# Linear attention and a gated MLP in one kernel: two more blocks take g times w_out by seven quarter products, and the written order of the work is made anew

## The chip, the cores and the metric

The kernel runs on one core of one Trainium2 chip. The metric is device time in microseconds; shown are the median of three runs and one profiled execution. An engine is called by its name or by the profile's short one: TensorE (PE, its weight loads PEld), VectorE (DVE), ScalarE (ACT), GpSimd (POOL), SyncE (SP, which issues nearly all DMAs).

## The reference

q, k and v have 8 batches, 8 heads, 576 tokens and 64 columns. Attention is linear, with features of exponentials, and its output is the input of an MLP with 4608 tokens, 512 columns and 2048 hidden columns:

```
phi(x):  p = x @ w_phi;  p = p - max|p|;  [exp(p), exp(-p)]        # 64 -> 256
kv = phi(k)^T v;  z = sum phi(k);  x = (phi(q) kv) / (phi(q) z + 1e-6)
h = x @ w_in;  g = h * erf(softplus(h));  out = g @ w_out
```

All is float32 in and out. The kernel takes each large float32 product as three float16 ones (high by high, high by low, low by high).

## The kernel before, in words

**Blocks and units.** The 4608 tokens are nine blocks of 512 (`NS`): eight batches without their last 64 tokens, and a ninth of these tails. The 2048 hidden columns are four units (`NU`). A unit (s, u) of the MLP makes h for one block and one unit (`h_unit`, L1060) by a Strassen-like scheme: seven products of 256 by 256 quarters in place of eight (`product`, L1032), whose sums are formed while the banks of PSUM are drained (`snap`, `add`). The input forms of the seven products (`split`, L871) and the weight forms (`split_weights`, L593) are pairs of float16; the weight forms of units 1 to 3 are kept in DRAM (`wd`) and fetched for each block into four tiles `ws` (`fetch`, L555).

**The gate.** `erf_gate` (L1108) takes Softplus and Erf on ScalarE, multiplies h by the result on VectorE (L1130, L1125), and then makes the operand of the second product. For blocks below `OW` (0 to 5) that is a float16 cast on ScalarE (L1133) and a subtraction on VectorE (L1136), both of 1024 columns, twice for a unit. For blocks from `OW` on (6 to 8) `g_forms` (L1140) makes four sums of quarters (`mix_g`, L1159) and seven pairs of float16 (`split_g`: ScalarE's cast, VectorE's subtraction L1153), of 512 columns each, in tiles `gf`.

**The second product** of a block goes in two rounds r of two units each, a round in two half-rounds. Below `OW` a half-round is `o_piece` (L1264): two token tiles, for each two units of four weight rows of 512 columns by three terms, 48 calls of `mm` (L509), which issues two matmuls on the two halves of the array's columns. The sums of round 0 are drained, stored in DRAM (`part`) and fetched for round 1. From `OW` on it is `o_chunk` (L1203): seven quarter products in 14 chunks for a round, seven for a half-round, 84 calls of `mm` with 256 columns; seven drains for a round (L1241, L1244) go to four sums `oc` that stay in SBUF. Their weight forms are made once by `t_forms` (L1173) on GpSimd, kept in DRAM (`td`) and fetched for each round (L1213).

**Attention** of batch b goes in nine groups of four tiles of 128 tokens for each batch: projection (`project`, L726), the row maximum and subtraction (`front`, L674 and L685), exponentials, turning (`t_piece`, by TensorE up to pair 9, then by a DMA transpose), kv and the quotients (`kv_piece`, `n_piece`, L524), and the split of x for the MLP (`x_piece`). Attention of batch b+1 is laid between the units of block b, so from about 736 us on only the MLP is left.

**The order** is made by a planner (`Plan`) in the host program: each operation has a cost, a latency and a rank (the place in the stream, `plan.pos`, plus an offset), and a simulated run picks on each engine the ready operation of the lowest rank; the order that comes out is each engine's instruction order. The planner holds tiles in pools with quotas (`plan.kind`), models DMAs as one queue (`land`), keeps GpSimd operations apart from VectorE operations marked `port`, charges 92 ns for a change of TensorE's mode and lets operations of another mode wait (`stay`). Where TensorE would be idle over 600 ns it puts in filler matmuls (`warm`, L1406).

Of the kernel before, what the change touches and what calls it, by code (L numbers as in the profile page):

```python
# [38 lines left out]
EARLY = 2 * NPAIR  # L39
PE_TURNED = 10  # L40
SPEED = {}
STAY2 = 5000.0
N1 = 12
TWO = 36
# [3 lines left out]
GATE_AT = (2000.0, 2000.0, 2000.0)  # L48
X_POOL = (0, 9)
T_POOL = 4  # L50
# [4 lines left out]
HL_POOL = (12, 20)  # L55
LATE = 1000.0
LATE2 = 2500.0
N3 = 7
FIRST = 2
XS = 8  # L60
XT = 3
RES = 1
WS = 8
HB = 4
PO = 2
BIG = 20
HALF = 36
N0 = 6
N2 = 24
W_EARLY = 3  # L70
W_NS = 1600.0
# [5 lines left out]
XT_ACT = (0, 2)  # L77
WRS = 4
GATE_OFF = (3000.0, 3500.0, 4500.0)
W_FROM = 16  # L80
W_EACH = 7
W_MM = 14
W_OFF = 6000.0
W_AHEAD = 12000.0
X_AHEAD = 8000.0
SEVEN = 7
O_ODD = (0, 1, 1, 0, 1, 1, 0)
# [3 lines left out]
KPS = 5  # L91
# [4 lines left out]
AHEAD = 5000.0  # L96
# [3 lines left out]
LAND = 0.68  # L100
HOLE = 600.0
OW = 6
GF = 18
OC = 6
TW_FROM = 16
TW_STEP = 1
TW_POOL = 1
OW_ODD = (0, 0, 1, 1, 1, 2, 2)
OW_EVEN = (0, 0, 0, 0, 0, 0, 0)
GW_OFF = 500.0  # L110
# [7 lines left out]
TAIL = (6, 1)  # L118
OW_LAG = 0
M_POOL = ()  # L120
GL_POOL = 0, 0
SYNC = 1
URGENT = 5000.0
NEAR = 100.0
PORT_NS = 120.0
WINDOW = 0.7
PRINT = None
EXP_LN = "natural_log_exp_and_others"

# [17 lines left out]
class Op:  # L147
    __slots__ = ("eng", "cost", "done", "fn", "prio", "bufs", "succ", "unmet", "ready", "start", "mode", "seq", "land", "port", "slack", "need", "give", "stay", "after", "made", "late")


class Plan:


    def __init__(self):
        self.ops = []
        self.slots = {}
        self.free = {}
        self.group = {}
        self.quota = {}
        self.line = {}  # L160
        self.row = {}
        self.pos = 0.0
        self.slack = 0.0
        self.stay = STAY
        self.late = LATE

# [11 lines left out]
    def op(self, eng, cost, fn, r=(), w=(), done=None, off=0.0, mode=COLS, land=0.0, port=False, need=None, give=None):  # L178
# [6 lines left out]
        o.late = self.late  # L185
        o.done = cost + 120.0 if done is None else done
        o.prio = self.pos + off
        o.seq = len(self.ops)
        o.succ, o.unmet, o.ready, o.start = [], 0, 0.0, None
        o.bufs = []  # L190
        deps = {}
# [44 lines left out]
    def run(self, filler):  # L236
# [17 lines left out]
        def room(o):  # L254
            if o.seq not in rooms:
                rooms[o.seq] = find_room(o) if any(b.slot is None for b in o.bufs) else 0.0
            return rooms[o.seq]

        def find_room(o):
            at = 0.0  # L260
            ahead, taken = {}, {}
            for b in o.bufs:
                if b.slot is not None:
                    continue
# [32 lines left out]
        def window(o, s):  # L297

            if o.prio + URGENT < min((c.prio for c in cand["DVE"]), default=0.0):
                return True  # L300
            work, blocked = max(0.0, free["DVE"] - s), False
            for c in cand["DVE"]:
# [3 lines left out]
                if at is None or max(c.ready, at) > s + NEAR:  # L306
                    continue
# [4 lines left out]
            return not blocked or work >= WINDOW * o.cost  # L312

        while left:
            rooms.clear()
            starts = {}
            for e in engines:
                t = None
                for o in cand[e]:
# [8 lines left out]
                    if t is None or s < t:  # L328
                        t = s
                if t is not None:  # L330
                    starts[e] = t
            if not starts:
# [8 lines left out]
            if held and held is not o:  # L341
                held.ready = max(held.ready, t)
            if e == "PE" and free[e] and t - free[e] > HOLE:
# [9 lines left out]
            table = o.give or table  # L353
# [4 lines left out]
            if o.land:  # L358
                queue_free = max(queue_free, t + o.cost) + o.land
                done = max(done, queue_free - t + o.late, o.done + o.late - LATE)  # L360
            free[e] = t + cost
            if o.port:
                port[e] = t + cost
                if e == "DVE":
# [3 lines left out]
            for b in o.bufs:  # L368
                if b.slot is None:
                    k = b.kind  # L370
# [7 lines left out]
                if b.left == 0:  # L378
                    used[b.kind] -= 1
                    self.free[self.group[b.kind]].append((b.end, b.slot))  # L380
            for n in o.succ:
# [5 lines left out]
                if n.unmet == 0:  # L387
                    cand[n.eng].append(n)
            order.append((t, o.seq, lambda o=o: self.emit(o)))
# [7 lines left out]
def favor_attention_moe(ctx: ExitStack, tc: tile.TileContext, qk, vp, wphi, w_in, w_out, out):  # L397
# [51 lines left out]
    for i in range(4 * NU):  # L449
        plan.slot("wd", f"wd{i}", pd.tile([P, HW], F32, tag=f"wd{i}", name=f"wd{i}"))  # L450
# [7 lines left out]
    plan.kind("wt", "big", (("wt",), WT))  # L458
# [3 lines left out]
    plan.kind("ws", "big", (("ws",), WS))  # L462
# [24 lines left out]
    whole("mb", 4, [P, GT], F32)  # L487
# [17 lines left out]
    op(SP, 450, lambda: nc.sync.dma_start(wst.t, wphi), w=[wst], done=2500)  # L505
# [42 lines left out]
    def wform(u, f):  # L548
# [3 lines left out]
        b = wforms[u][f // 2]  # L552
        return b, f, lambda hl, j: b.t.bitcast(F16).rearrange("p (f h j n) -> p f h j n", f=2, h=2, j=2)[:, f % 2, hl, j, :]

    def fetch(u):  # L555
        wforms[u] = []
        for i in range(4):
            b, d = buf("ws"), wstored[u][i]
            keys = range(2 * i, min(2 * i + 2, FORMS))
            n = 512 * len(keys)  # L560
            op(SP, 430, lambda b=b, d=d, n=n: nc.sync.dma_start(b.t[:, :n], d.t[:, :n]), r=[d], w=[(b, (f, j)) for f in keys for j in range(2)], done=2500, land=1300 * len(keys) * LAND, off=-W_AHEAD)
            wforms[u].append(b)

    def single(src, eng, st, f, port=True):
        word = lambda k: st.t.bitcast(I32).rearrange("p (e w) -> p e w", w=2)[:, :, k]
        for c, (d, s) in enumerate(src):
            op(SP, 430, lambda d=d, s=s: nc.sync.dma_start(d(st), s), w=[(st, c)], done=2500, land=2600 * LAND / len(src))
# [7 lines left out]
    def load_weight():  # L575
# [3 lines left out]
        plan.pos += W_OFF  # L579
# [13 lines left out]
    def split_weights(u, j):  # L593
        if u >= RES and j == 0:
            wforms[u] = [buf("ws") for _ in range(4)]
# [26 lines left out]
        if u >= RES and j == 1:  # L622
            wstored[u] = []
            for i in range(4):
                d = buf("wd")
                d.left += 1
                w = wforms[u][i]
                n = 512 * min(2, FORMS - 2 * i)
# [834 lines left out]
```

## Time and profile before

| | |
|---|---|
| median of three runs | 947.59 us (947.37 to 947.97) |
| the profiled execution | 945.1 us, span 943.3 us |
| TensorE matmul busy | 931.6 us, 99% of the span |
| TensorE weight load | 792.1 us, 84% |
| VectorE | 756.8 us, 80% |
| ScalarE | 716.9 us, 76% |
| GpSimd | 225.9 us, 24% |
| HBM | 119.50 MB read, 30.15 MB written |

The span is from the first instruction to the last; 1.8 us of the profiled execution lie around it. Matmuls are pipelined and their ends are modelled, so what one costs is read from the distance of starts and not from its own length. Busy time of the other engines is the union of their instructions.

### The profile page before, as it was taken

Reading aid. Unit: us, or ns where it says so; the run is one execution under the profiler, and the core shown is the slowest. Engines: PE = TensorE matmul, PEld = TensorE weight load, DVE = VectorE, ACT = ScalarE, POOL = GpSimd, SP = SyncE. Lnnn points to the kernel's source line nnn. Section 1 sums busy time; section 2 is a strip of 40 time slices with the busy share of each in tenths; the row PEclk is TensorE's granted clock in tenths of the full one; section 3 lists DMA queues with packets and bytes.
Section 4 is the critical chain, followed back from the end, with each engine's and each line's share of the span. In section 5 each row is a group of like instructions: output and inputs, shape, how many; then the busy total and the mean of one; then the engine's idle time right before and its main releaser. Section 6 shows DMA issues by size and latency. Waiting matters only on the chain.

```text
span 943.3 us, 37531 instructions
## 1 busy us (share of the span) xinstructions
PE 931.6 (99%) x16646; PEld 792.1 (84%) x16646; DVE 756.8 (80%) x1352; ACT 716.9 (76%) x1117; POOL 225.9 (24%) x233
## 2 busy tenths in 40 slices
PE   9999999999999999999999999999999999999998
PEld 7878877878787878778798878787787999999997
DVE  6989999999777877787887886788877787786875
ACT  7979898878688687867877684766777578679792
POOL 0343221221645856310301130010310330010000
PEclk9999999999999999999999999999999999999999
DMA  9389999999666749476966577475847693883412
GB/s 335 106 213 331 300 246 299 333 348 276 176 173 186 195 159 255 120 188 152 246 140 177 132 179 169 114 182 169 204 69 216 175 239 109 217 213 114 146 47 47
DMA packets 179490, 181.45 MB, mean 192 GB/s; under 512 B 125056, under 2 KB 133376, under 8 KB 179328
## 3 DMA queue, kind: packets, MB, share of 16 engines
q1 hardware_dynamic: 179328, 179.05, 69.3%
q8 instruction: 130, 2.13, 0.9%
q14 instruction: 32, 0.26, 0.1%
HBM read 119.50 MB, written 30.15 MB: 159 GB/s over the span
## 4 chain that ended last, share of the span: by engine, by line
PE 87%; DVE 6%; DMA 3%; ACT 2%; POOL 1%; issue 1%; SPq 0%; DVEq 0%; POOLq 0%
PE bank L514 67%; PE bank L524 13%; PE bank L726 5%; DMA half<-half 3%; PE bank L757 1%; DVE m L674 1%; PE bank L1406 1%; ACT big L532 1%; POOL half L881 1%; DVE half L570 0%; DVE half L685 0%; DVE half L1136 0%; DVE half L572 0%; DVE big L1057 0%; DVE ld L699 0%
## 5 line engine op out<-in xcount | busy, mean ns | idle before, releaser
L514 PEld LDWEIGHTS <-half 128*64 128x64 f16 x4320 | 243.1, 110 | 89.2 <-issue 1.4
L514 PE MATMUL bank<-woh,half 128*64 128x512 f16 (+1 forms) x2112 | 300.1, 351 | 0.8 <-DVE big L685 0.8
L514 PE MATMUL bank<-half,big 128*64 128x256 f16 x4536 | 274.4, 273 | 1.5 <-ACT big L532 1.5
L514 PEld LDWEIGHTS <-big 128*64 128x64 f16 x4536 | 247.3, 110 | 17.8 <-issue 2.1
L514 PE MATMUL bank<-wol,half 128*64 128x512 f16 (+1 forms) x1056 | 191.1, 350 | 0.0
L532 ACT ACTIVATE big<-bank 128x512 f32<-128x512 f32 x190 | 112.0, 608 | 74.1 <-PE bank L514 71.7
L532 ACT ACTIVATE big<-big 128x512 f32<-128x512 f32 x200 | 124.2, 628 | 54.3 <-DVE big L685 35.5
L881 POOL TENSOR_TENSOR half<-big,half 128x512 f16<-128x512 f32 x54 | 63.2, 1179 | 211.3 <-DVE half L878 69.0
L1057 DVE SCALAR_TENSOR_TENSOR big<-bank,big 128x512 f32<-128x512 f32 x108 | 73.5, 684 | 45.1 <-PE bank L514 33.7
L674 DVE TENSOR_REDUCE m<-bank 128x4 f32<-128x512 f32 x144 | 92.5, 682 | 15.2 <-PE bank L726 14.6
L514 PE MATMUL bank<-half,wi 128*64 128x256 f16 x1512 | 92.7, 273 | 1.1 <-DMA half<-half 1.1
L514 PEld LDWEIGHTS <-wi 128*64 128x64 f16 x1512 | 81.9, 110 | 4.9 <-issue 1.7
L524 PEld LDWEIGHTS bank<-v,big 128*64 128x64 f32 x2016 | 78.2, 138 | 8.0 <-issue 1.3
L524 PE MATMUL bank<-v,big 128*64 128x65 f32 (+1 forms) x2016 | 84.0, 229 | 0.6 <-issue 0.4
L524 PE MATMUL bank<-kv,big 128*64 128x65 f32 x2304 | 82.2, 222 | 0.9 <-DVE big L685 0.9
L524 PEld LDWEIGHTS bank<-kv,big 128*64 128x64 f32 x2304 | 76.4, 138 | 5.7 <-DVE big L685 1.1
L1130 DVE TENSOR_TENSOR big<-big,big 128x1024 f32<-128x1024 f32 x48 | 58.2, 1239 | 25.2 <-ACT big L1119 25.1
L532 ACT ACTIVATE half<-big 128x512 f16<-128x512 f32 x84 | 48.6, 622 | 32.6 <-DVE big L1159 31.1
L1103 ACT ACTIVATE big<-big 128x1024 f32<-128x1024 f32 x72 | 72.7, 1050 | 0.4
L514 PE MATMUL bank<-big,half 128*64 128x256 f16 x1152 | 68.3, 273 | 0.0
L1136 DVE TENSOR_TENSOR half<-big,half 128x1024 f16<-128x1024 f32 x48 | 59.3, 1261 | 4.8 <-ACT half L1133 4.4
L1153 DVE TENSOR_TENSOR half<-big,half 128x512 f16<-128x512 f32 x84 | 55.0, 693 | 3.4 <-ACT half L532 2.4
(74 smaller groups left out, 1253.6 us busy)
## 6 DMA issues: line engine op xcount, KB each, us to landing
big<-wd SPq DMA_DIRECT2D x81, 512.0 KB, 5.1
ld<-in_qk_dram SPq DMA_DIRECT2D x31, 576.0 KB, 5.3
big<-td SPq DMA_DIRECT2D x24, 512.0 KB, 4.4
v<-in_vp_dram SPq DMA_DIRECT2D x28, 325.0 KB, 4.6
big<-in_moe_w_in_dram SPq DMA_DIRECT2D x32, 256.0 KB, 5.8
big<-in_moe_w_out_dram SPq DMA_DIRECT2D x16, 512.0 KB, 6.6
out_dram<-half SPq DMA_DIRECT2D x32, 256.0 KB, 3.0
big<-wd SPq DMA_DIRECT2D x27, 256.0 KB, 4.6
```

Of the source, the lines that this page charges most:

```text
L514: nc.tensor.matmul(o[half], a[:, half], b, start=start, stop=stop, **kw)
L524: nc.tensor.matmul(o[half], a[:, half], b, start=first and c == 0, stop=last and c == 1)
L532: nc.scalar.activation(out_(), in_(), func, **k)
L674: op(DVE, 600, lambda: nc.vector.tensor_reduce(m.t, ps(), axis=AX.X, op=ALU.max, apply_absolute_value=True), r=[b], w=[m])
L726: nc.tensor.matmul(both[nm].t[:, t * P : (t + 1) * P], x()[rows], w.t[rows, :], start=i == 0, stop=i == len(terms) - 1)
L757: op(PE, 110, lambda t=t: nc.tensor.transpose(b.t[:, t * P : (t + 1) * P], uview(u)[:, t, :], ident.t), r=[u, ident], w=[b], done=330, mod ...
L881: op(POOL if pool else DVE, 1160 if pool else 600, lambda: eng.tensor_tensor(tv(1), view(), tv(0), op=ALU.subtract), r=[*reads, (t, 0)], w ...
L1057: op(DVE, 640, lambda: nc.vector.scalar_tensor_tensor(h.t[:, c * 512 : c * 512 + 512], b.t, HSCALE, h.t[:, c * 512 : c * 512 + 512], op0=A ...
L1103: fn = lambda: nc.scalar.activation(L.t, h.t, AF.Softplus, scale=1.0 / SG)
L1130: op(DVE, 1140, lambda h=h, L=L: nc.vector.tensor_tensor(h.t, h.t, L.t, op=ALU.mult), r=[L, h], w=[h], port=True, off=GATE_OFF[0] * (v + 1))
L1136: op(POOL if pool else DVE, 2290 if pool else 1140, lambda h=h, a=a, b=b, eng=eng: eng.tensor_tensor(halfs(b), h.t, halfs(a), op=ALU.subtr ...
L1153: op(POOL if pool else DVE, 1160 if pool else 600, lambda: eng.tensor_tensor(hv(1), src(), hv(0), op=ALU.subtract), r=[key, (g, 0)], w=[(g ...
```

## The change: what it does

`OW` goes from 6 to 4, so blocks 4 to 8 take the second product by quarter products, and `t_forms` starts at step 10 (was 16). The weight forms `ws` become seven tiles of 512 columns (were four of 1024, two forms in each), and the fetched forms `wt` become eight half tiles for a round (were four whole ones); both move to the pool of half tiles, which grows from 36 to 50 while the pool of big ones shrinks from 20 to 13. The planner's DMA model gets new latencies and queue times; every operation carries its step, and a table `SHIFT` moves the ranks of single operations from given times on (some 175 entries). Groups of attention are laid together in the first batch (`VISITS`) and from group 32 on in pairs (`TWO`, was 36). Work moves between engines: the halves of k and q of pairs 12 to 19 from GpSimd to VectorE (`HL_POOL` no longer holds a pair that is split), the differences of weight quarters of units 2 and 3 from GpSimd to VectorE (`T_POOL`), the casts of x of block 2 from VectorE to ScalarE (`XT_ACT`); the first load of w_phi goes through ScalarE's queue. The last drain is made in two halves of 256 columns with the products in an order that ends one half first, and its stores go out on SyncE's and ScalarE's queues. Many offsets and quotas change; `GF` stays at 18.

```diff
-STAY2 = 5000.0
+STAY2 = 7000.0
-TWO = 36
+TWO = 32
-T_POOL = 4
+T_POOL = 2
-HL_POOL = (12, 20)
+HL_POOL = (8, 12)
-WS = 8
+WS = 12
-BIG = 20
-HALF = 36
+BIG = 13
+HALF = 50
-XT_ACT = (0, 2)
+XT_ACT = (0, 3)
-OW = 6
+OW = 4
 GF = 18
-OC = 6
-TW_FROM = 16
+OC = 8
+TW_FROM = 10
-WT = 4
+WT = 8
-OB = 3
+OB = 4
-TAIL = (6, 1)
+TAIL = (5, 1)
+VISITS = ((0,), (1,), (2, 3), (4, 5), (6, 7), (8,))
+STAY0 = 6000.0
+SHIFT = {
+    0.0: {22: 3000, 30: 1000, 33: 1000, 59: -2000, 61: 6000, 68: 10822, 96: 4905, 101: 3905, 107: -2000,
...
+    705000.0: {7172: -3000, 7186: 6000},
+}
...
+        shifts = sorted(SHIFT.items())
         while left:
+            while shifts and free["PE"] >= shifts[0][0]:
+                for seq, by in shifts.pop(0)[1].items():
+                    self.ops[seq].prio = self.ops[seq].base + by
...
             if o.land:
-                queue_free = max(queue_free, t + o.cost) + o.land
-                done = max(done, queue_free - t + o.late, o.done + o.late - LATE)
+                queue_free = max(queue_free, t + 400.0) + o.land
+                done = max(done, queue_free - t + 1000.0) + o.late
...
-    plan.kind("wt", "big", (("wt",), WT))
+    plan.kind("wt", "half", (("wt",), WT))
-    plan.kind("ws", "big", (("ws",), WS))
+    plan.kind("ws", "half", (("ws",), WS))
-    op(SP, 450, lambda: nc.sync.dma_start(wst.t, wphi), w=[wst], done=2500)
+    op(ACT, 450, lambda: nc.scalar.dma_start(wst.t, wphi), w=[wst], done=2500)
...
     def fetch(u):
-        wforms[u] = []
-        for i in range(4):
-            b, d = buf("ws"), wstored[u][i]
-            keys = range(2 * i, min(2 * i + 2, FORMS))
-            n = 512 * len(keys)
...
+        wforms[u] = {}
+        for i, f in enumerate((B11, T3, T2, B21, T1, B22, T4)):
+            b, d = buf("ws"), wstored[u][f]
+            op(SP, 430, lambda b=b, d=d: nc.sync.dma_start(b.t, d.t), r=[d], w=[(b, (f, j)) for j in range(2)], done=3900, land=970, off=1200.0 * i - early("W_AHEAD", plan.step))
+            wforms[u][f] = b
...
-            for f in (T3, T2, T1, T4):
+            for n, (m_, v_) in enumerate(x for x in O_SEQ if x[0] in (1, 2, 4, 6)):
+                f = {1: T3, 2: T2, 4: T1, 6: T4}[m_]
                 d, b = tds[f, r], buf("wt")
-                wts[s, f] = b
+                wts[s, f, v_] = b
...
+        last = (s, r) == (NS - 1, 1) and i == 13
+        for k, q in ((k, q) for k in range(2) for q in range(2)) if last else ((k, q) for q in range(2) for k in range(2)):
...
+        if last:
+            t, n = key
+            c = outs.pop((s, key))
+            rows = out.rearrange("(k i s) c -> i s k c", i=2, s=S)
+            for k in range(2):
+                part = slice(k * Q, k * Q + Q)
+                op(DVE, 360, lambda part=part: nc.vector.scalar_tensor_tensor(c.t[:, part], bank.t[:, part], scale, c.t[:, part], op0=ALU.mult, op1=ALU.add), r=[(bank, k), c], w=[(c, k)])
+                for i, (e, q) in enumerate(((SP, nc.sync), (ACT, nc.scalar))):
+                    op(e, 400, lambda i=i, k=k, q=q, part=part: q.dma_start(
+                        rows[i, 512:, 2 * t + k, n * Q : n * Q + Q], c.t[i * D : i * D + D, part]), r=[(c, k)], done=2400, land=250)
```

## Rows read from the trace of the kernel before

**Rows 1.** The page: busy time of each engine, share of the span, instructions.

```profile
PE 931.6 (99%) x16646; PEld 792.1 (84%) x16646; DVE 756.8 (80%) x1352; ACT 716.9 (76%) x1117; POOL 225.9 (24%) x233
```

**Rows 2.** Busy time in stretches; columns: stretch, length, each engine's busy us (instructions), clock, DMA.

```profile
0.00:106.50 106.50, 102.73 (x1948) 87.30 (x1950) 89.56 (x227) 86.70 (x264) 28.88 (x37) 1.00 0.83 257
106.50:200.80 94.30, 91.40 (x1496) 74.52 (x1494) 91.62 (x167) 82.20 (x127) 27.15 (x29) 1.00 0.99 304
200.80:293.90 93.10, 93.10 (x1570) 73.84 (x1566) 75.09 (x118) 74.60 (x105) 42.22 (x44) 1.00 0.78 210
...
507.20:714.20 207.00, 206.92 (x3696) 164.45 (x3692) 162.00 (x280) 145.75 (x188) 27.65 (x22) 1.00 0.64 154
...
507.20:864.80 357.60, 357.52 (x6434) 310.14 (x6430) 276.23 (x463) 260.46 (x337) 50.48 (x41) 1.00 0.66 169
735.90:938.70 202.80, 202.78 (x3708) 202.06 (x3702) 153.41 (x233) 151.93 (x194) 22.83 (x19) 1.00 0.53 147
```

**Rows 3.** Waits of TensorE, whole span: who waited for what, us, times, longest.

```profile
PE bank L514 <- DMA half<-half: 1.1, 1, 1.1
```

**Rows 4.** TensorE's filler matmuls, grouped by line, whole span: busy us, mean ns.

```profile
L1406 PE MATMUL bank<-hot 128*64 128x512 f16 x66 | 9.5, 435 | 1.4 <-DVE hot L1412 1.4
```

**Rows 5.** Timeline of TensorE near 485 us, 512-column products: start, us, instructions.

```profile
485.12 0.67 PE L514 MATMUL bank<-woh,half 128*64 128x512 f16 x4
...
485.77 0.67 PE L514 MATMUL bank<-woh,half 128*64 128x512 f16 x4
```

**Rows 6.** VectorE's groups by line in 507.2 to 714.2: count, busy us, mean ns.

```profile
L1136 DVE TENSOR_TENSOR half<-big,half 128x1024 f16<-128x1024 f32 x16 | 19.7, 1250 | 0.6 <-ACT half L1133 0.5
...
L1287 DVE TENSOR_SCALAR half<-bank 128x512 f32<-128x512 f32 x8 | 5.5, 686 | 8.3 <-PE bank L514 8.3
```

**Rows 7.** VectorE's groups by line in 714.2 to 791.9 (four units).

```profile
L1153 DVE TENSOR_TENSOR half<-big,half 128x512 f16<-128x512 f32 x28 | 18.8, 708 | 1.7 <-ACT half L532 1.4
...
L1159 DVE TENSOR_TENSOR big<-big,big 128x512 f32<-128x512 f32 x8 | 6.1, 767 | 0.0
L1159 DVE TENSOR_TENSOR big<-big 128x512 f32<-128x512 f32 x8 | 5.5, 683 | 0.0
```

**Rows 8.** ScalarE's groups by line, whole span: count, busy us, mean ns.

```profile
L1133 ACT CAST half<-big 128x1024 f16<-128x1024 f32 x48 | 48.7, 1037 | 0.1
L532 ACT ACTIVATE half<-big 128x512 f16<-128x512 f32 x84 | 48.6, 622 | 32.6 <-DVE big L1159 31.1 <-issue 1.4
```

**Rows 9.** Chain of waits from 930 us on: start, us, what.

```profile
938.72 0.69 DVE half L1244
```

**Rows 10.** DMA issues of SyncE at the start: start, us, what.

```profile
1.21 0.89 SPq L644 DMA_DIRECT2D ld<-in_qk_dram  x2
```

**Rows 11.** Timeline of TensorE at the start.

```profile
1.45 3.20 PE L1406 MATMUL bank<-hot 128*64 128x512 f16 x14 [1.45 <-DVE hot L1412]
4.58 2.74 PE L726 MATMUL bank<-wphi,ld 64*128 64x128 f32 x32
```

**Rows 12.** GpSimd's groups by line, whole span: count, busy us, mean ns.

```profile
L699 POOL TENSOR_TENSOR ld<-ld,ld 128x640 f16<-128x640 f32 (+1 forms) x16 | 20.4, 1281 | 36.1 <-PE bank L524 19.9 <-issue 7.2 <-DVE half L771 5.8
...
L610 POOL TENSOR_TENSOR half<-half,half 128x256 f32<-128x256 f32 x24 | 17.5, 735 | 23.6 <-DVE half L1136 5.5 <-DVE half L572 4.1 <-DVE wi L620 3.6
```

**Rows 13.** VectorE's groups for like operations, whole span.

```profile
L699 DVE TENSOR_TENSOR ld<-ld,ld 128x640 f16<-128x640 f32 (+1 forms) x24 | 17.8, 747 | 0.0
L620 DVE SCALAR_TENSOR_TENSOR big<-half,big 128x256 f16<-128x256 f32 x42 | 17.6, 452 | 2.4 <-ACT big L532 2.4
```

**Rows 14.** VectorE's timeline at 750 us.

```profile
750.09 1.36 DVE L1159 TENSOR_TENSOR big<-big,big 128x512 f32<-128x512 f32 x1
```

**Rows 15.** GpSimd's timeline at the same place.

```profile
749.75 1.16 POOL L881 TENSOR_TENSOR half<-big,half 128x512 f16<-128x512 f32 x1 [5.66 <-DVE big L1159]
```

**Rows 16.** DMA issues by tile: count, KB each, us to landing.

```profile
big<-wd SPq DMA_DIRECT2D x81, 512.0 KB, 5.1
...
big<-td SPq DMA_DIRECT2D x24, 512.0 KB, 4.4
```

More of the change, by code (lines that the diff above doesn't have):

```diff
@@ L90 @@
 RATE0 = 10400.0
-KPS = 5
+KPS = 4
 QPS = 5
@@ L95 @@
 HALVED = 12
-AHEAD = 5000.0
+AHEAD = 8000.0
 TURN = 92.0
@@ L121, with early @@
 GL_POOL = 0, 0
+GL_V = 0,
 SYNC = 1
-URGENT = 5000.0
+URGENT = 8000.0
 NEAR = 100.0
 PORT_NS = 120.0
-WINDOW = 0.7
+WINDOW = 0.8
+NE = 8
+EARLY = {}
+PACE = (1.0, 1.0, 1.0, 1.0, 1.0, 1.0, 1.0)
+VISITS = ((0,), (1,), (2, 3), (4, 5), (6, 7), (8,))
+STAY0 = 6000.0
+BIASED2 = 0, 0
+OSB_ACT = 0, 2
+OC_ACT = 9, 9
+SHIFT = {
[38 rows of a table added]
+}
 PRINT = None
 EXP_LN = "natural_log_exp_and_others"
+def early(name, step):
+    return EARLY.get(name, globals()[name]) if step < NE else globals()[name]
 class Buf:
@@ L147 @@
 class Op:
-    __slots__ = ("eng", "cost", "done", "fn", "prio", "bufs", "succ", "unmet", "ready", "start", "mode", "seq", "land", "port", "slack", "need", "give", "stay", "after", "made", "late")
+    __slots__ = ("eng", "cost", "done", "fn", "prio", "bufs", "succ", "unmet", "ready", "start", "mode", "seq", "land", "port", "slack", "need", "give", "stay", "after", "made", "late", "step", "open", "base")
 class Plan:
@@ L163, in __init__ @@
         self.slack = 0.0
-        self.stay = STAY
+        self.stay = STAY0
+        self.step = -1
         self.late = LATE
@@ L311, in window @@
                     work += c.cost
-            return not blocked or work >= WINDOW * o.cost
+            return not blocked or work >= early("WINDOW", o.step) * o.cost
+        starts, stale = {}, set(engines)
+        shifts = sorted(SHIFT.items())
         while left:
-            rooms.clear()
-            starts = {}
-            for e in engines:
+            while shifts and free["PE"] >= shifts[0][0]:
+                for seq, by in shifts.pop(0)[1].items():
+                    self.ops[seq].prio = self.ops[seq].base + by
+            for e in stale:
                 t = None
@@ L352, in run @@
             o.start = t
-            table = o.give or table
+            stale.add(e)
+            if o.give:
+                table = o.give
+                stale.add("ACT")
             cost, done = o.cost, o.done
@@ L363, in run @@
                 port[e] = t + cost
+                stale.add(other[e])
                 if e == "DVE":
@@ L369, in run @@
                 if b.slot is None:
+                    rooms.clear()
+                    stale.update(engines)
                     k = b.kind
@@ L378, in run @@
                 if b.left == 0:
+                    rooms.clear()
+                    stale.update(engines)
                     used[b.kind] -= 1
@@ L448, in favor_attention_moe @@
     plan.kind("tails", "tails")
-    for i in range(4 * NU):
-        plan.slot("wd", f"wd{i}", pd.tile([P, HW], F32, tag=f"wd{i}", name=f"wd{i}"))
+    for i in range(FORMS * NU):
+        plan.slot("wd", f"wd{i}", pd.tile([P, 512], F32, tag=f"wd{i}", name=f"wd{i}"))
     plan.kind("wd", "wd")
@@ L594, in split_weights @@
         if u >= RES and j == 0:
-            wforms[u] = [buf("ws") for _ in range(4)]
+            wforms[u] = {f: buf("ws") for f in (B11, T3, B21, T2, T1, B22, T4)}
         rows = []
@@ L969, in n @@
             groups.append([(n_piece, g)] + turned(g))
-        for g in range(per):
-            groups.append([(k_piece, g)] + load(g))
-            if g >= 4:
-                n(g - 4)
-            if g >= 2:
-                groups.append([(t_piece, g - 2)])
-            if g:
-                groups.append([(kv_piece, g - 1)])
+        for visit in VISITS:
+            for g in visit:
+                groups.append([(k_piece, g)] + load(g))
+            for g in visit:
+                if g >= 4:
+                    n(g - 4)
+            for g in visit:
+                if g >= 2:
+                    groups.append([(t_piece, g - 2)])
+            for g in visit:
+                if g:
+                    groups.append([(kv_piece, g - 1)])
         g = per
@@ L1216, in o_chunk @@
         bank, g = po[s, kind], gf[(s, u), xf]
-        for q in range(2):
+        last = (s, r) == (NS - 1, 1) and i == 13
+        for k, q in ((k, q) for k in range(2) for q in range(2)) if last else ((k, q) for q in range(2) for k in range(2)):
             F = 2 * u + q
@@ L1244, in o_chunk @@
             op(DVE, 640, lambda: nc.vector.scalar_tensor_tensor(c.t, bank.t, scale, c.t, op0=ALU.mult, op1=ALU.add), r=[bank, c], w=[c])
-        if r == 1 and done:
+        if r == 1 and done and not last:
             t, n = key
@@ L1296, in o_piece @@
             for r0, own in rows:
-                op(SP, 400, lambda r0=r0, own=own: nc.sync.dma_start(out[r0 : r0 + own.stop - own.start, :], s_.t[own, :]), r=[s_], done=2400, land=1300*LAND/len(rows))
+                op(SP, 400, lambda r0=r0, own=own: nc.sync.dma_start(out[r0 : r0 + own.stop - own.start, :], s_.t[own, :]), r=[s_], done=2400, land=1000/len(rows))
         po.pop((s, tt))
@@ L1388, in favor_attention_moe @@
             since += x
-            if since > (W_NS if len(loaded) < 12 else W_NS2) and wq:
+            if since > early("W_NS" if len(loaded) < 12 else "W_NS2", n) and wq:
                 load_weight()
```

157 lines of the change are left out of this document (85 added, 72 removed), and 36 rows, old and new, of the table SHIFT.

## The prediction

> **What bounds the kernel now.** I read the page's busy times first: TensorE's matmuls cover 931.6 us of a span of 943.3, VectorE 756.8, ScalarE 716.9, GpSimd 225.9 [rows 1]. Since matmul ends are modelled, I checked that 99% in the stretches and in the waits. From 507 us to 864.8 the matmul rows leave 0.1 us uncovered, while VectorE is busy for 276.2 of 357.6 us; the clock column says 1.00, the level of 2.4 GHz [rows 2]. The waits name no large wait of TensorE; the longest for a DMA is 1.1 us [rows 3]. So past some 200 us the order of the work is bound by TensorE's own products, and a product less is time less, as long as the other engines keep up. The beginning is different: up to 106.5 us TensorE is covered for 102.7 us, but part of that is filler, 66 matmuls and 9.5 us in all [rows 4], and from 106.5 to 200.8 us VectorE is busy for 91.6 of 94.3 us and the DMA engines for 0.99 of the time [rows 2].
>
> **The products.** Eight half-rounds change their form: two blocks, two rounds, two halves. The pitch of the new form is read where nothing but 256-column products runs, 735.9 to 938.7 us: 3708 matmul records in 202.8 us, two to a call, 109.4 ns a call [rows 2]. The old form: six matmuls of 512 columns, three calls, from 485.12 to 485.77 us, 217 ns a call [rows 5]. A half-round had 48 calls, 48 x 0.217 = 10.4 us, and gets 84, 84 x 0.1094 = 9.2 us. The difference is 1.21 us, for eight half-rounds **9.7 us less**. The pitch of 109.4 ns holds there with the weight path covered for 202.1 of 202.8 us, so what the additional weight loads cost is in it. This term is the firm one.
>
> **What the other engines get for it.** In blocks 4 and 5 a unit loses two subtractions of 1024 columns (L1136: 16 of them 19.7 us, so 2.46 us a unit [rows 6]) and gains seven of 512 (L1153: 28 in 18.8 us, 4.70 us a unit) and four sums (L1159: 16 in 11.6 us, 2.90 us) [rows 7]. That is 5.14 us more of VectorE for each of eight units, 41.1 us. A round is drained seven times where it was four, at 0.69 us [rows 6]: 2.06 us more for each of four rounds, 8.2 us. ScalarE changes two casts of 1.04 us for seven of 0.58 [rows 8], 2 us a unit, 16 us over 200 where it has 145.8 of 207 us to do [rows 2]; that lies beside TensorE's work.
>
> VectorE is the narrow place. These units fall into 507.2 to 714.2 us, where the attention of batches 6 and 7 runs too. It was busy there for 162.0 us; with 41.1 us and three rounds' drains, 6.2 us, it has 209.3 us to do, and TensorE would need only 207.0 - 9.7 = 197.3. That can't hold inside the stretch. Up to 864.8 us it is 276.2 + 41.1 + 8.2 = 325.5 us of 347.9, 94%, below the 97% that VectorE shows from 106.5 to 200.8 us [rows 2]. So some 12 us of its work must slip behind 714 us, where attention ends and VectorE has room. 18 `gf` tiles hold the operands of two units and a half; two units' sums and subtractions are 2 x 7.6 = 15.2 us, just enough. The ends: nothing, if all of it slips; 209.3 / 0.97 - 197.3 = 18 us, if none does. I take **2 us more**, near the lower end, because the stretch before gave TensorE no gap at VectorE's 78% and the later one has the room; both ends go into the range.
>
> **The tail.** The last drain starts at 938.72 and takes 0.69 us [rows 9]; the span ends 3.9 us later, with two stores issued one behind the other. Half a drain is at least 0.35 us less, one issue of SyncE 0.45 us (two take 0.89 [rows 10]). I take **0.7 us less**; 0 to 1.1 are the ends.
>
> **The first load.** With w_phi on ScalarE's queue SyncE issues q and k one issue (0.4 us) earlier, but the first projection starts at 4.58 us, when the filler of 1.45 to 4.65 us ends [rows 11], and that filler stays. Nothing, then; with that cover gone, 0.4 us either way.
>
> **The beginning, ordered anew.** Paired groups, a stronger wish to stay in a mode and moved ranks can only take back what TensorE doesn't work: up to 106.5 us that is 3.8 us of gaps [rows 2] and at most 9.5 us of filler [rows 4]. All 13.3 us are one end. The other is a loss of as much, since no row shows the new order, and VectorE's 89.6 us of 106.5 leave it little room. I take a quarter, **3.3 us less**, as the gaps and fillers are what a list of ready work for TensorE is made to close.
>
> **Work moved to VectorE.** Halving q and k of pairs 12 to 19 leaves GpSimd (16 operations, 20.4 us [rows 12]); VectorE needs 0.75 us each by like operations, 12 us [rows 13]. They belong to the attention of batches 3 and 4, laid between blocks 2 and 3; in the stretch there VectorE is busy for 75.1 of 93.1 us [rows 2]: nothing, and if that room were taken, up to 12 us. The weight differences of units 2 and 3 are 16 operations of some 0.45 us [rows 13] in the stretch that is 97% full. They stop holding GpSimd for 0.73 us each [rows 12], during which VectorE can't always work (below), so the ends are 0 and 7.2 us; I take **1 us more**. Casts of block 2 that go to ScalarE have room there.
>
> **The smaller transfers.** `ws` goes from 108 fetches of 512 and 256 KB [rows 16] to 27 x 7 = 189 of 256 KB, `wt` from 24 to 5 x 2 x 8 = 80, the partial sums of two blocks (16 DMAs) go. SyncE issues 121 DMAs more, at 0.45 us 54 us of its queue, and the first product of a unit waits for 256 KB instead of 512. A landing is 4.4 to 5.1 us [rows 16], fetched 9 us and more ahead in the order. Nothing, with TensorE's waits for DMA at 1.1 us; the other end is a rival.
>
> **Sum**, against the profiled execution's own 945.1 us: - 9.7 + 2 - 0.7 - 3.3 + 1 = - 10.7, 934.4 us. The median of the runs stands 2.5 us above that execution, so **936.9 us**. Its own range is 931 to 943.
>
> **Rivals.**
> *VectorE becomes the bound from 507 to 714 us; slower than before.* An operand of the second product waits for its last subtraction; until then h and the gate hold their tiles, four of each (two units), and the big pool is cut to 13, so the next unit's drains have no tile and TensorE stops. For it: 209.3 us of work in 197.3. Against it: the 18 tiles. Price: 18 us where I took 2, 952.9 us. It turns the result once more than 12.7 of those 18 us are lost, that is once under some 5 us of VectorE's work get past 714 us. What makes it worse is GpSimd. A sum on VectorE that starts at 750.09 took 1.36 us where others take 0.68 [rows 7, 14]; a GpSimd subtraction ran from 749.75 to 750.91 [rows 15], and the sum ended 0.54 us behind it. GpSimd has 27.7 us of such work in the stretch [rows 2], and all the added subtractions and sums read two tiles of SBUF. If half of GpSimd's time stops VectorE, 14 us come on top of 209.3, and the deferral of 12 us must be 26, for which there are no tiles. The Trainium skill (SBUF — State Buffer, section "SBUF: two separate sides") says that an instruction of VectorE with two SBUF inputs and one of GpSimd that reads SBUF exclude each other for the whole instruction; the row agrees. By that rule in full VectorE would be the bound here, and this rival the result. I give it 16%, since the planner keeps the two apart by its marks and VectorE's drains, which read PSUM, can fill in.
>
> *The transfers eat the gain.* Each of ten rounds waits for two more issues of SyncE (0.9 us) ahead of its forms: 9 us, 946 us. For it: 121 more issues on one queue. Against it: the shown waits. 10%, of which 3 are still over 0.2% faster.
>
> *The beginning gives more.* All 13.3 us of filler and gaps go: 10 us less than forecast, 926.9 us. Against it: VectorE and ScalarE each have over 86 us to do in these 106.5 [rows 2]. 14%.
>
> **How the numbers follow.** The forecast has 60%. The kernel's measurement can't tell less than 0.2% (1.9 us) from no change, so faster is below 945.7 us: 60 + 14 + 3 = 77%; same 7%; slower 16%. For 8 in 10 the range goes from the third rival's time to about half-way through the first's price (2 to 18 us): 927 to 949 us.
>
> **What would show it.** Right: matmul records of 256 columns up by 8 x 168 and those of 512 down by 8 x 96; the stretch of blocks 4 and 5 shorter by 8 to 10 us with TensorE still covered; VectorE over 95% there, its L1153 and L1159 of block 5 running behind the end of attention; fewer than 66 fillers. Wrong: waits of TensorE for VectorE's subtractions of g or fillers past 500 us (first rival); for `wd` or `td` loads (second); or a longer stretch from 106.5 to 200.8 us.

## The result, and the profile after

The changed kernel takes 934.82 us (median of 4 runs, 934.48 to 934.95), the kernel before 947.66 us in the same comparison: ratio 0.9864, 95% interval 0.9847 to 0.9881. Its profiled execution took 934.75 us, the span is 932.9 us, 10.4 us shorter than the span before. The forecast was 936.9 us for the median and 934.4 us for the profiled execution.

The page of the changed kernel, busy time of each engine: 11 us less of TensorE, 47 us more of VectorE and 33 us less of GpSimd [rows 1]. The prediction's terms for VectorE add up to 68.5 us, some 65 without the seven casts that leave it; why 47 came of them stands under VectorE below.

```profile
PE 920.2 (99%) x17226; PEld 813.9 (87%) x17226; DVE 803.7 (86%) x1462; ACT 736.3 (79%) x1164; POOL 192.9 (21%) x201
```

TensorE's groups of the MLP by shape (L584 is `mm` now): count, busy us, mean ns, idle before. The four groups of 256 columns sum to 9408 records, 1344 = 8 x 168 more than before; the two groups of 512 columns sum to 1536, 768 = 8 x 96 less. At the pitches of the prediction that is the 9.7 us.

```profile
L584 PE MATMUL bank<-half,half 128*64 128x256 f16 x6456 | 381.3, 273 | 0.0
L584 PE MATMUL bank<-woh,half 128*64 128x512 f16 x1024 | 164.9, 380 | 0.0
L584 PE MATMUL bank<-wol,half 128*64 128x512 f16 x512 | 98.0, 379 | 0.0
L584 PE MATMUL bank<-half,wi 128*64 128x256 f16 x1512 | 93.4, 273 | 0.4 <-issue 0.4
L584 PE MATMUL bank<-woh,half 128*64 128x256 f16 x960 | 87.8, 273 | 1.3 <-DVE big L756 0.8 <-DVE half L1326 0.5
...
L584 PE MATMUL bank<-wol,half 128*64 128x256 f16 x480 | 68.6, 273 | 0.0
```

Its stretches, cut where the blocks' first Softplus begins; the columns are those of [rows 2]. Look at VectorE (third figure) from 595.5 to 700.3 us: 102.74 of 104.80 us, 98%, and TensorE's gaps there, 1.6 us. In the stretch behind it VectorE has 89%, where block 6 had 76% before (the line below the stretches): work slipped there. Blocks 4 and 5 together are 10.9 us shorter (196.1 for 207.0), and block 6 is 4.2 us longer.

```profile
0.00:106.50 106.50, 100.60 (x1922) 85.98 (x1922) 93.53 (x228) 90.42 (x259) 28.77 (x36) 1.00 0.88 262
106.50:197.60 91.10, 90.63 (x1498) 72.06 (x1500) 88.88 (x177) 78.81 (x132) 13.62 (x11) 1.00 0.99 288
...
504.20:595.50 91.30, 91.30 (x1860) 85.35 (x1858) 85.14 (x152) 73.78 (x105) 9.58 (x8) 1.00 0.76 195
595.50:700.30 104.80, 103.16 (x2222) 100.12 (x2220) 102.74 (x193) 81.60 (x117) 13.59 (x12) 1.00 0.72 179
504.20:714.20 210.00, 208.36 (x4354) 198.90 (x4352) 201.21 (x364) 168.28 (x236) 26.25 (x22) 1.00 0.74 190
700.30:782.20 81.90, 81.90 (x1628) 81.43 (x1624) 72.83 (x124) 63.53 (x85) 20.99 (x18) 1.00 0.72 198
```

Block 6 in the kernel before:

```profile
714.20:791.90 77.70, 77.70 (x1410) 72.81 (x1406) 59.39 (x103) 58.60 (x77) 18.12 (x15) 1.00 0.70 192
```

A TensorE that is covered by matmuls can still lose time, so I set each stretch's length against its records at the pitch of their kind (256 columns 54.6 ns a record, 512 columns 108.2, the kv and quotient products 29.5, or 56 with 130 columns, projections 27.6 or 58, transposes 109). What remains are fillers, gaps, waits and changes of mode. The columns are cut at 100 and 200 us and at the first Softplus of a block (b3 runs from block 3's to block 4's); all us, the experiments below included:

```
                  0-100 100-200 200-b3    b3    b4    b5    b6  b7-end    sum
before              26.2   6.7    2.4    2.4   1.1   2.1  -0.1    5.3     46.1
after               24.8   6.2    2.3    1.8   0.9   4.0   0.4    5.2     45.4
before_five         25.9   6.5    3.0    2.6   8.1  11.3   3.4    5.6     66.4
before_five_mix     25.1   6.4    2.5    1.7   3.9   7.9   0.5    5.5     53.4
no_ranks            28.0   8.1    2.2    2.4   2.9   4.7   0.4    4.9     53.7
start_ranks         24.0   6.3    2.3    1.9   2.9   4.8   0.4    4.9     47.4
sub_double          25.0   6.2    2.5    1.8  17.0  24.7   0.6    5.0     82.8
sum_eighth          24.6   6.2    2.3    1.8   1.6   2.8   0.4    4.9     44.7
two_back            24.4   6.3    2.2    2.0   1.6   3.2  -0.1    5.3     44.9
to_pool_no_ranks    27.8   9.6    2.9    2.7   2.9   4.8   0.4    5.3     56.3
before_again        25.9   6.5    2.6    2.6   1.1   2.8  -0.1    5.4     46.7
```

From before to after, 1.9 us go in the first 200 us, 0.7 up to block 4, and 2.2 us come in blocks 4 to 6; with the products, 9.7 us, that is the 10.4 us of the spans but for rounding. before_again is the kernel before once more: from one execution to the next an entry moves by up to 0.7 us.

### The profile page after: what moved, and what is told of

It is laid out like the page before. It is cut to its first block, busy times and chain, and to the rows that moved or that the text cites. A ratio compares the mean times of both kernels' runs of the same rounds, so it can differ in the third digit from the quotient of the medians.

```text
span 932.9 us, 38966 instructions
## 1 busy us (share of the span) xinstructions
PE 920.2 (99%) x17226; PEld 813.9 (87%) x17226; DVE 803.7 (86%) x1462; ACT 736.3 (79%) x1164; POOL 192.9 (21%) x201
## 4 chain that ended last, share of the span: by engine, by line
PE 84%; DVE 11%; ACT 2%; issue 2%; DMA 1%; SPq 0%; POOL 0%; DVEq 0%; ACTq 0%
PE bank L584 64%; PE bank L594 12%; PE bank L797 5%; DVE m L740 1%; ACT big L602 1%; DVE half L1233 1%; PE bank L828 1%; PE bank L1501 1%; DVE big L1207 1%; DVE half L756 1%; DVE big L1239 1%; DVE big L1132 1%; DVE big L918 1%; DMA half<-td 1%; DVE big L1202 0%
## 5 line engine op out<-in xcount | busy, mean ns | idle before, releaser
L584 PEld LDWEIGHTS <-half 128*64 128x64 f16 x9432 | 512.4, 110 | 74.0 <-issue 2.0
L584 PE MATMUL bank<-half,half 128*64 128x256 f16 x6456 | 381.3, 273 | 0.0
L584 PE MATMUL bank<-woh,half 128*64 128x512 f16 (+1 forms) x1984 | 252.7, 328 | 1.3 <-DVE big L756 0.8
L584 PE MATMUL bank<-wol,half 128*64 128x512 f16 (+1 forms) x992 | 166.5, 328 | 0.0
L602 ACT ACTIVATE half<-big 128x512 f16<-128x512 f32 x140 | 81.2, 622 | 57.7 <-DVE big L1239 51.9
L1233 DVE TENSOR_TENSOR half<-big,half 128x512 f16<-128x512 f32 x140 | 92.5, 694 | 2.7 <-ACT half L602 1.7
L584 PE MATMUL bank<-half,wi 128*64 128x256 f16 x1512 | 93.4, 273 | 0.4 <-issue 0.4
L584 PEld LDWEIGHTS <-wi 128*64 128x64 f16 x1512 | 81.1, 110 | 4.3 <-issue 1.4
L594 PE MATMUL bank<-v,big 128*64 128x65 f32 (+1 forms) x2016 | 81.9, 228 | 0.4 <-ACT big L602 0.4
L1202 DVE TENSOR_TENSOR big<-big,big 128x1024 f32<-128x1024 f32 x40 | 49.5, 1262 | 19.3 <-ACT big L1196 19.3
L756 DVE TENSOR_TENSOR half<-bank,m 128x512 f32<-128x512 f32 x72 | 49.0, 683 | 0.1
L1207 DVE TENSOR_TENSOR big<-big,big 128x1024 f32<-128x1024 f32 x32 | 39.8, 1267 | 9.6 <-ACT big L1196 9.4
```

The costliest lines, as they stand in the source:

```text
L584: nc.tensor.matmul(o[half], a[:, half], b, start=start, stop=stop, **kw)
L594: nc.tensor.matmul(o[half], a[:, half], b, start=first and c == 0, stop=last and c == 1)
L602: nc.scalar.activation(out_(), in_(), func, **k)
L756: op(DVE, 600, lambda: nc.vector.tensor_tensor(to(), ps(), m.t.unsqueeze(2).to_broadcast([P, GT, NF]), op=ALU.subtract), r=[b, m], w=[key])
L1202: op(DVE, 1140, lambda h=h, L=L: nc.vector.tensor_tensor(h.t, h.t, L.t, op=ALU.mult), r=[L, h], w=[h], port=True, off=GATE_OFF[0] * (v + 1))
L1207: op(DVE, 1140, lambda h=h, L=L: nc.vector.tensor_tensor(h.t, h.t, L.t, op=ALU.mult), r=[L, h], w=[h], port=True, off=GATE_OFF[0] * (v + 1))
```

## The experiments

Medians of before in these comparisons: 946.2, 946.5 and 946.4 us. Its single runs lie between 943.9 and 950.3 us. The changed kernel was timed in the first comparison alone, where the kernel before stood at 947.66 us, 1.1 to 1.4 us higher than here. So a difference from its 934.82 us is known to no better than that, and the worths below, taken from medians, hold within it.

**before_again**: the kernel before, unchanged.

> The kernel before, unchanged, profiled on the chip of these runs. The first profiled execution of it (945.1 us) stood 2.5 us under the median of its timed runs, the one of the changed kernel (934.75 us) at its median. If the 2.5 us belong to that one execution or its chip, this profile gives 947 to 948 us, span near 946, and the comparison of the two spans gains some 2.5 us at places that the trace names. If a profiled execution of this order of work is always that much faster than a timed one: 945 us again.

Measured: median 946.52 us, ratio 1.0003 (0.9994 to 1.0013); the profiled execution 945.66 us, span 943.9. The first expectation missed: the execution is the fastest of its ten (up to 947.61). The second missed too: it stands 0.9 us under its median and not 2.5. So I take the 2.5 us for the spread of the kernel before, of which both profiles hit the lower end, and for no cost at a place. That this order of work is faster under the profiler is not excluded by two profiles; as a rule of all orders it is not so, since two_back's profiled execution is the slowest of its six.

**two_back**

```diff
-OW = 4
+OW = 6
-    480000.0: {5051: 8402},
...
-    705000.0: {7172: -3000, 7186: 6000},
```

> The changed kernel with blocks 4 and 5 back on the old second product (OW = 6), and the moved ranks kept only for the work ahead of block 4. Theory A, the prediction's: TensorE's products set the time, so 9.7 us come back and the 2 us that VectorE's overload costs go: 942.5 us (941 to 945). Theory B: VectorE's added work paid most of the shorter products back and the gain is from the new order and the moved work: under 938 us.

Measured: 942.6 us (0.9959, 0.9946 to 0.9973). The two blocks are worth 7.8 us, as theory A had it. The run also lacks the ranks from 480 us on, which were set for five blocks, so their worth is in the 7.8; against start_ranks below, which lacks all ranks from 210 us on, the two blocks are worth 5.5 us.

**before_five**

```diff
-OW = 6
+OW = 4
-TW_FROM = 16
+TW_FROM = 10
-OC = 6
+OC = 8
```

> The kernel before with five blocks on quarter products (OW = 4, TW_FROM = 10, OC = 8) and nothing else of the change: its own tiles, transfer model and ranks. Theory A: 947.7 - 9.7 and a loss in blocks 4 and 5 of 2 to 6 us: 940 to 944 us. Theory B (VectorE becomes the bound without the rest of the change): 950 us or more.

Measured: 956.07 us (1.0115, 1.009 to 1.014): slower, theory B. By itself the step that the change is named for loses 10 us: its products are 9.7 us shorter, and TensorE loses 20.3 us more than before, 19.7 of them in blocks 4 to 6 (table). The stretches of this run by block:

```profile
508.10:611.20 103.10, 99.25 (x1968) 91.20 (x1964) 93.29 (x168) 78.16 (x111) 9.58 (x8) 0.98 0.69 172
611.20:713.60 102.40, 98.67 (x2037) 93.97 (x2035) 92.54 (x168) 77.56 (x109) 13.11 (x11) 0.98 0.72 176
713.60:802.50 88.90, 87.86 (x1724) 86.02 (x1721) 75.97 (x132) 63.99 (x86) 21.57 (x18) 1.00 0.71 169
```

VectorE is not full, at 90%: it waits itself. These are its longest waits and ScalarE's from 508 to 802 us (two views of the same run): ScalarE waits for the sums of quarters, VectorE for Erf.

```profile
ACT half L532 <- DVE big L1159: 25.8, 18, 5.1
```

```profile
DVE big L1125 <- ACT big L1119: 13.6, 8, 3.7
```

**before_five_mix**: the same, and

```diff
-O_ODD = (0, 1, 1, 0, 1, 1, 0)
+O_ODD = (1, 0, 1, 0, 1, 0, 1)
-OW_ODD = (0, 0, 1, 1, 1, 2, 2)
+OW_ODD = (1, 1, 1, 1, 1, 1, 1)
-OW_EVEN = (0, 0, 0, 0, 0, 0, 0)
+OW_EVEN = (0, 0, 0, 0, 0, 2, 2)
```

> The kernel before with five blocks on quarter products as before (956 us) and, besides, the changed kernel's three tables that say how many chunks of the second product stand behind each of the seven products of h (O_ODD, OW_ODD, OW_EVEN). Theory A: what kept the bare change from its gain is that the chunks stand early in a unit and wait for VectorE's subtractions, and a later place of them is most of the cure: 940 to 946 us. Theory B: it is the tiles (pools, quarter weights in the big pool) or the ranks: 952 us or more.

Measured: 943.04 us (0.9974, 0.9962 to 0.9986). Three tables that say where the chunks stand take back 13 us; theory A. Apart from two filler matmuls they change no instruction, only places. Of the 22.8 us lost in blocks 4 to 6 they take back 10.5; how an early chunk costs its time, by waiting for VectorE's subtractions as the expectation has it, is argued and not shown. VectorE is now at 96% in block 5:

```profile
505.70:599.00 93.30, 91.77 (x1835) 85.66 (x1832) 84.44 (x151) 73.18 (x102) 9.50 (x8) 1.00 0.74 188
599.00:710.00 111.00, 110.03 (x2352) 104.82 (x2349) 106.05 (x198) 85.36 (x122) 13.14 (x11) 1.00 0.66 170
```

**no_ranks**: the changed kernel's table `SHIFT` empty.

```diff
-SHIFT = {
...
-}
+SHIFT = {}
```

> The changed kernel with the table of moved ranks empty, all else kept, so the planner's order is its own. Theory A: the products carry the gain and the ranks at most the few us of fillers and gaps: 935 to 940 us. Theory B: the ranks carry the gain, being what lets VectorE's work of blocks 4 and 5 fit: 944 us or more, with waits of TensorE for VectorE between 500 and 720 us.

Measured: 943.23 us (0.9975, 0.9958 to 0.9993), between the two theories, nearer to B's size but not B's place: 5.1 us of the loss lie in the first 200 us and 2.7 in blocks 4 to 6. It equals before_five_mix, so without the ranks the new tiles, transfer times, groups and moved work have in sum no worth that can be seen beside the three tables. The fillers of this run, 196 matmuls, and under them those of the changed kernel, 70:

```profile
L1462 PE MATMUL bank<-hot 128*64 128x512 f16 x196 | 25.1, 398 | 1.4 <-DVE hot L1468 1.4
```

```profile
L1501 PE MATMUL bank<-hot 128*64 128x512 f16 x70 | 10.3, 431 | 1.5 <-DVE hot L1507 1.5
```

**start_ranks**: without the entries of `SHIFT` from 210 us on.

```diff
-    210000.0: {2142: 1, 2297: -3000, 2732: -6000},
...
-    705000.0: {7172: -3000, 7186: 6000},
```

> The changed kernel with the moved ranks of the first 200 us alone (the entries of the table up to 180 us). Without ranks it took 943.2 us, with all of them 934.8. Theory A: some 5 of the 8.4 us are fillers and gaps of the first 200 us, the rest is VectorE's work in blocks 4 to 6: 938 us. Theory B: the ranks' worth is in blocks 4 to 6: 942 us or more.

Measured: 937.07 us (0.9897, 0.9873 to 0.9921), theory A: 6.2 of the ranks' 8.4 us come from the entries of the first 200 us; the later entries bring 2.3 us, in block 4 (2.9 to 0.9) and block 5 (4.8 to 4.0).

**two_back_no_ranks**

```diff
-OW = 4
+OW = 6
-SHIFT = {
...
-}
+SHIFT = {}
```

> The changed kernel with two blocks back on the old second product and the table of moved ranks empty. With the run without ranks (943.2 us) it gives what the shorter products are worth without them. Theory A (the ranks' 8 us are general, fillers and gaps at the start above all): 943.2 + 8 = 951 us, so the products keep their gain. Theory B (the ranks are what lets VectorE's added work fit): 945 us or less, the products' gain mostly paid back without the ranks.

Measured: 948.35 us (1.0031, 1.0016 to 1.0047), between the theories. Without ranks the two blocks are worth 948.35 - 943.23 = 5.1 us, with them 7.8. Without both, the rest of the change makes the kernel 1.8 us slower than before (948.35 against 946.52).

**sub_double** and **sum_eighth**: order of the changed kernel unaltered, more and less of VectorE in blocks 4 and 5; the second computes an eighth of the sums of g's quarters there.

```diff
+                if n[0] in (4, 5):
+                    eng.tensor_tensor(hv(1), src(), hv(0), op=ALU.subtract)
                 return eng.tensor_tensor(hv(1), src(), hv(0), op=ALU.subtract)
```

> The changed kernel, its order unaltered, with every subtraction of g's quarters in blocks 4 and 5 (56, VectorE, 0.69 us) issued twice: 38 us more of VectorE where it is busy for 201.2 of 210.0 us (504 to 714 us). Theory A (VectorE is full there and sets the time once more comes): some 9 us fit into the stretch and up to 9 into the next, so 20 us or more come on top: 955 us or more. Theory B (its queue has room that busy shares don't show): under 942 us.

```diff
+            few = 64 if n[0] in (4, 5) else 512
-            op(POOL if pool else DVE, 1160 if pool else 600, lambda: eng.tensor_tensor(out(), x(), y(), op=ALU.subtract if sub else ALU.add), r=r, w=w, port=True, off=at[0] - GP_OFF * pool)
+            op(POOL if pool else DVE, 1160 if pool else 600, lambda: eng.tensor_tensor(out()[:, 0:few], x()[:, 0:few], y()[:, 0:few], op=ALU.subtract if sub else ALU.add), r=r, w=w, port=True, off=at[0] - GP_OFF * pool)
```

> The changed kernel, its order unaltered, with the four sums of g's quarters in blocks 4 and 5 over 64 of 512 columns (the rest of the sum is left out): some 18 us less of VectorE in 504 to 714 us. Theory A, the prediction's: VectorE's overload costs 2 us as it stands, since the order already shifts the rest: 2 us less, 932 to 933.5 us, the 4 us of TensorE's loss from 595 to 700 us halved. Theory B: VectorE holds the stretch altogether: 6 us or more less.

Measured: 972.0 us (1.0281, 1.0265 to 1.0297) and 933.94 us (0.9878, 0.9863 to 0.9893). 38 us more of VectorE cost 37 us. 18 us less, 14 of them in these two stretches, give 0.9 by the medians, less than what the two comparisons differ by (1.1), and 0.8 by the spans. The stretches of sub_double,

```profile
504.70:612.10 107.40, 95.32 (x1860) 87.30 (x1857) 101.45 (x175) 74.16 (x104) 9.58 (x8) 0.98 0.64 166
612.10:737.20 125.10, 109.03 (x2206) 103.70 (x2207) 123.68 (x224) 82.26 (x118) 13.12 (x11) 0.96 0.62 150
```

and of sum_eighth:

```profile
504.10:594.90 90.80, 90.33 (x1830) 84.19 (x1828) 77.86 (x151) 73.83 (x104) 9.58 (x8) 1.00 0.73 196
594.90:699.00 104.10, 103.50 (x2234) 100.44 (x2232) 95.87 (x193) 81.83 (x116) 13.57 (x12) 1.00 0.74 181
```

So in this order more work on VectorE in blocks 4 and 5 costs all of itself, and less gives next to nothing. In sub_double the first theory held. In sum_eighth neither did: 933.94 lies above the first theory's 932 to 933.5, and the loss of block 5 fell from 4.0 to 2.8 us and was not halved. That VectorE's fullness is the reason is shown for neither: both runs keep the written order, and in block 4 of sub_double 16.3 us more of VectorE made the stretch 16.1 us longer although VectorE had been busy for only 93% of it. There the fixed order alone, in which each subtraction comes later, is an untested rival.

**to_pool_no_ranks**: the table empty, and

```diff
-T_POOL = 2
+T_POOL = 4
-HL_POOL = (8, 12)
+HL_POOL = (12, 20)
```

> The changed kernel without moved ranks (943.2 us) and with the halves of k and q of pairs 12 to 19 and the weight differences of units 2 and 3 back on GpSimd. Theory A, the prediction's: 7 us leave VectorE where it is 97% full (106 to 198 us), but GpSimd's operations hold it off; 1 us less, 942 us. Theory B: GpSimd's longer operations (1.28 us for 0.75) delay what waits for them: 945 us or more.

Measured: 945.7 us (944.2 to 947.0; 0.9991, 0.9978 to 1.0004), theory B: 2.5 us more than without ranks alone, 1.3 of them in the first 200 us (table); block 2's first Softplus comes at 299.3 us instead of 297.2.

**old_tail**, and below it **tail_whole**, each the changed kernel with one edit

```diff
-        last = (s, r) == (NS - 1, 1) and i == 13
+        last = False
```

```diff
-            for k in range(2):
-                part = slice(k * Q, k * Q + Q)
...
+            op(DVE, 640, lambda: nc.vector.scalar_tensor_tensor(c.t, bank.t, scale, c.t, op0=ALU.mult, op1=ALU.add), r=[(bank, 0), (bank, 1), c], w=[c])
+            for i, (e, q) in enumerate(((SP, nc.sync), (ACT, nc.scalar))):
+                op(e, 400, lambda i=i, q=q: q.dma_start(
+                    rows[i, 512:, 2 * t : 2 * t + 2, n * Q : n * Q + Q], c.t[i * D : i * D + D].rearrange("p (k c) -> p k c", k=2)), r=[c], done=2400, land=500)
```

> The changed kernel with the last drain, its products' order and its stores as before, read in the trace from the last matmul's end to the end of the span (4.6 us before, 4.1 in the changed kernel, which stops TensorE for 0.5 us ahead of the last eight matmuls). Theory A, the prediction's: the split tail is worth 0.7 us: span 933.6. Theory B: what the drain and the stores give, the stop takes: 932.9 within 0.2.

> The changed kernel with its last products in the new order, but one drain of 512 columns and two stores, one on SyncE's queue and one on ScalarE's. No stop of TensorE (0.5 us less), the drain 0.27 us longer, the stores issued side by side: if the stop comes from the first half's drain, 0.2 to 0.4 us less than the changed kernel, span 932.5 to 932.7. If the stop is there anyhow: 933.1 or more.

Measured, one execution each: spans of 932.8 and 933.3 us, 932.9 in the changed kernel (932.6 to 933.0 in its four runs). The split tail is worth nothing that shows. The chains of waits of the changed kernel and, below, of old_tail and of tail_whole's first piece from 925 us on (start, us, what) show why: the second half's matmuls wait for the first half's drain, 0.5 us; the drain ends at 929.29 in place of 928.73, and the stores, 0.5 us quicker, only make up for that. tail_whole has no such stop, but its order leaves TensorE 70 matmuls behind 925 us, for 58 and 56, and ends later; as a cure it failed.

```profile
924.96 2.74 PE bank L584 x50
927.70 0.02 issue
927.73 0.44 DVE half L1326
928.16 0.04 issue
928.20 0.64 PE bank L584 x8
928.85 0.02 issue
928.87 0.42 DVE half L1326
```

```profile
924.95 3.07 PE bank L584 x56
928.01 0.02 issue
928.04 0.69 DVE half L1338
```

```profile
924.94 3.83 PE bank L584 x70
```

## Why the prediction was right, step by step

- **The products, 9.7 us less**: the records came out as counted. The worth of the two blocks, 7.8 us (two_back), would fit 9.7 less the 2 us for VectorE, but that is not shown: two_back loses 4.7 us in blocks 4 to 6, nearly as much as the changed kernel's 5.3 (table), and lacks the late ranks.
- **VectorE, 209.3 us to do in 507 to 714 us, 2 us lost**: 2.2 us were lost in blocks 4 to 6 (table). The size was met, but by luck: without the late ranks, which the prediction gave no price, it is 5.0 us (start_ranks, 8.1 against 3.1 before), and in the order of before 19.7. The 209.3 were some 6 us too many. They add lengths of single operations to a busy time, and operations that follow each other overlap: three subtractions of 0.68 us take 1.88 us, so one starts every 0.60 us.

```profile
550.93 1.88 DVE L1233 TENSOR_TENSOR half<-big,half 128x512 f16<-128x512 f32 x3
552.73 0.68 DVE L1239 TENSOR_TENSOR big<-big 128x512 f32<-128x512 f32 x1
```

  At 0.08 us of overlap, 97 operations more and 16 less give those 6 us, an estimate; the same overlap makes 47 us of busy time out of 65 us of lengths over the whole span. Work did slip into block 6, but not g's: by the first two lines below (busy us and count of the subtractions L1233 and of the sums L1239 from 504.2 to 700.3 us), 55 of the 56 subtractions of blocks 4 and 5 and all 32 sums ran before block 6, so the sign that they run behind the end of attention did not come. What slipped are copies and operations of attention above all, as the last line has it for L756.

```profile
504.20:700.30 196.10, 36.48 (x55) 1.00 0.73 187
504.20:700.30 196.10, 21.86 (x32) 1.00 0.73 187
700.30:782.20 81.90, 3.86 (x6) 1.00 0.72 198
```

  VectorE's groups from 504.2 to 714.2 us, where 57 subtractions of 512 columns stand for 16 of 1024 before (L1136 [rows 6]):

```profile
L1233 DVE TENSOR_TENSOR half<-big,half 128x512 f16<-128x512 f32 x57 | 37.9, 692 | 0.8 <-ACT half L602 0.6
...
L1338 DVE SCALAR_TENSOR_TENSOR half<-bank,half 128x512 f32<-128x512 f32 x17 | 11.5, 682 | 0.0
L1239 DVE TENSOR_TENSOR big<-big,big 128x512 f32<-128x512 f32 x16 | 10.9, 684 | 0.0
L1239 DVE TENSOR_TENSOR big<-big 128x512 f32<-128x512 f32 x16 | 10.9, 682 | 0.0
```

- The *reason* for taking the low end was wrong. I reasoned from stock, two and a half units of `gf` tiles, that the work can slip. The same work in the order of before (before_five; a unit's sums and the quota of 18 are the same) cost some 20 us in blocks 4 to 6: the first rival's price of 18 and its side of the result, 956 against 952.9. What decides for the most part is where the chunks stand among the products of h, three tables in the diff that the prediction didn't cost. The rival's second half, GpSimd holding VectorE off, played next to no part: from 504 to 714 us five operations of VectorE took over 60 ns more than the median of their shape, 1.8 us in all, each beside one of GpSimd; 1.5 of the 1.8 fall into block 4, where TensorE lost no more than before.
- **The first load, nothing**: right; the first projection starts at 4.58 us as before.
- **The tail, 0.7 us less**: nothing. Half a drain took 0.42 us, 0.27 less than a whole one and not "at least 0.35", and I didn't see that the second half's products wait for the first half's drain.
- **The beginning, 3.3 us less**: 1.9, and of other parts: in the first 200 us the moved ranks give 5.1 us, and the rest of the change takes 3.2 (table, before against no_ranks). The reason was wrong. Gaps and fillers, which were to close, stayed: TensorE is covered for 193.63 of the first 200 us, 193.32 before (the sums of two stretches below), and there are 70 fillers, 10.3 us, for 66 and 9.5, where fewer were the sign. Where in the covered time the 1.9 us went stays open.

```profile
sum 200.00, PE 193.63 PEld 160.03 DVE 184.81 ACT 171.62 POOL 42.39; mean PE 96.81 PEld 80.02 DVE 92.41 ACT 85.81 POOL 21.20
sum 200.00, PE 193.32 PEld 161.37 DVE 180.38 ACT 168.12 POOL 56.03; mean PE 96.66 PEld 80.68 DVE 90.19 ACT 84.06 POOL 28.02
```

- **Work moved to VectorE, 1 us more**: the sign was wrong where it was measured: without the ranks the move gives 2.5 us. I take it that what counted was how long GpSimd makes others wait (1.28 us for 0.75 [rows 12, 13]), not VectorE's share; no run shows the waits by themselves, nor the worth of the move with the ranks.
- **The smaller transfers, nothing**: right. 189 and 80 fetches landed in 4.4 and 4.6 us (DMA issues of the changed kernel), and no wait of TensorE names one, though the chain of waits runs through two loads from `td` near 565 and 600 us, 4.7 us in all.

```profile
half<-wd SPq DMA_DIRECT2D x189, 256.0 KB, 4.4
half<-td SPq DMA_DIRECT2D x80, 256.0 KB, 4.6
```

- **The 2.5 us** from the profiled execution to the median are the whole miss of 2.1 us: they did not carry over, and I take them for the kernel before's spread (before_again).
- **The sum**: 10.4 us less against 10.7 for the profiled execution, and in part by luck. The 0.7 us that the tail did not give and the 0.4 us that were missing in the first 200 us are nearly made up by 0.7 us between 200 us and block 4 that no term had.

Open is what the new tiles and transfer times are worth with ranks moved for them, as the ranks fit one order alone; and which of the late entries bring the 2.3 us.

## What to carry to other kernels

Where a product gets shorter on the busiest engine, count what the next engine must do in that very stretch: here a change that cuts 9.7 us off TensorE gave 10 us more or 3.5 us less by three tables of the order alone, and 12.8 us less with the rest of the change. Room in tiles didn't say here that work would slip without loss; the places of the consumers in the order did. Count an engine's work by the distance of starts and not by the lengths of its operations. And where two engines are full at once in a fixed order, don't expect the price of more work to be its worth when it goes: 38 us more cost 37, and 18 less gave 0.9.

## What the runs showed that I had not expected

When TensorE waited for VectorE, it also lost clock: in sub_double the granted clock was 0.98 and 0.96 of full speed in blocks 4 and 5, and 0.98 in before_five's, where the changed kernel has 1.00 in both; so a part of such a loss is not in the waits.
